# A gated mix of attention and spectral filter: the output bank in two runs of channels, and another order of work at the head

## The chip, the cores and the metric

The kernel runs on one core of a Trainium2 chip. The time is the device time of one execution in microseconds; three runs gave 405.25, 405.87 and 407.12, with a median of 405.87. A profiled execution, from which all rows of the profile come, took 405.76; its span, from the first instruction to the last, is 404.0.

## The reference

Only the input x of branch A is used: both branches read it. `D` is 448, `S` 2048, sixteen heads of 28.

```python
x = A_x
g = _sigmoid((x * gate_w).sum(-1, keepdims=True))
a = _A_ref(x, A_wqkv, A_wo)          # softmax attention, 16 heads of 28
b = _B_ref(x, B_w_r, B_w_i)          # rfft2, times (w_r + 1j*w_i), irfft2, to bfloat16
return g * a + (1 - g) * b
```

```python
qkv = (lambda x, *d: x.transpose(*d))((x @ wqkv).reshape(B, S, 3, H, Dh), 2, 0, 3, 1, 4)
scores = jnp.einsum("bhqd,bhkd->bhqk", q, k) * scale
p = _softmax(scores, axis=-1)
o = jnp.einsum("bhqk,bhkd->bhqd", p, v)
return (lambda x, *d: x.transpose(*d))(o, 0, 2, 1, 3).reshape(B, S, D) @ wo
```

## The kernel before

**Tiling.** Four heads lie on the 128 partitions, each in 32 rows of which 28 hold data. A group is four heads by 512 queries: four groups of heads by four blocks of queries, 16 groups, numbered `n` (`plan_steps`). For each group there are 16 tiles of 128 keys, `kt`. A score tile is one head, one `kt` and 512 queries: `k` times `q` into one PSUM bank. Because the squares of the norms are carried in two spare rows of `q` and `k`, a score is a negative squared distance, and no row maximum is needed; the weights for it are put into `vw`.

**Exponentials.** Most score tiles go to ACT (L1302): three from `psA`, then two from `psB`, into a ring of 28 slots. The list `ND` (L533) says for each group how many of the 16 `kt` go to DVE instead: those are scored into a spare bank (`dunit`, L1250), turned into bit patterns of a power of two by one addition and maximum (L1256), and shifted to three further phases by POOL or DVE (L1268; `PHS[PHX]` says which engine). All four phases are summed by P times V with weights that average them. A tile on ACT costs one P-times-V quad, a tile on DVE four. `pvb` holds the sum over all keys of a group; `normalise` copies it out, inverts the row sums by way of DRAM, and POOL multiplies (L1453).

**Spectral branch** (`background`). It runs beside the attention: a transform over channels (`Bd`), over tokens (`A`, `CS`), the product with the weights, and back. Its result `zt` enters the output tiles.

**Output tiles.** For each of 16 tiles of 128 tokens, `out_mm` (L1462) adds eight terms into one bank: four spectral ones of 224 channels each (even or odd channels, hence a step of two in the bank) and four attention ones, one for each group of heads, with `wo_pad`. DVE copies the bank to `fin` and it goes to DRAM (`out_tile`); the last four tiles are made after the attention's end (`last_tile`), partly beforehand.

**Order.** The program writes out operations with a duration, a key and their dependences; `Sched.run` plays them through and hands out a fixed order for each engine, with due times from the constants at L176 to L194 and `Kernel.T0` to `TB`. PE, ACT, DVE, POOL and the loads on SP each follow their list. POOL operations and those on DVE marked `lk` are kept apart. Where PE would be idle for long, small matmuls of zeros are put in.

**Head** (`prologue`). The constants and the weights of the first four heads' keys go through ACT's queue, the first 512 tokens and the queries' weights through SP's. POOL clears and fills the padded weights `wpk`, DVE fills `wpq`. PE runs 20 matmuls of zeros, transposes the tokens into four banks (copied to `xT` by ACT and DVE in turn), and projects twice: once for the squares (ACT, L841), and once more into another bank, to which a selector matmul adds the norms; DVE scales the sum to `q` and `k` (L852). Queries go first as one piece of 512, keys as pieces of 128 and 384. Blocks 1 to 3 of the keys are made while the first exponentials run: `x_block` transposes, `proj_fast` projects (scale L1032, square L1038, selector matmul, addition L1048), `v_block` makes `vw` and the gate's logits (L1123).

Of the kernel before, what the change touches and what calls it, by code (L numbers as in the profile page):

```python
# [11 lines left out]
BF16 = mybir.dt.bfloat16  # L12
# [9 lines left out]
FN = 113  # L22
# [11 lines left out]
PHX = 1  # L34


def free_dims(ap, dims, offset=0):
    return _AP(tensor=ap.tensor, offset=ap.offset + offset,
               ap=[list(ap.ap[0])] + [list(d) for d in dims])

# [115 lines left out]
class Op:  # L156
    __slots__ = ("first", "last", "heat", "lk", "eng", "dur", "emit", "deps", "key", "rel", "mode", "acq", "free", "lat",
                 "start", "end", "name", "step", "n")
# [23 lines left out]
DUE_P = 7.01  # L182
SWP = 0.98
PVA, PVD = -2, 0.36
URG = 1
FLEAD = 4.66
SQPOOL = 0
EL, ELAST = 1.7, 4.49
NLD = 2
KP = 37.88  # L190
KN, KO, PLEAD, DSP, DHOLD, RWAIT, WREL, XLEAD, QLEAD, WLEAD = 0.77, 4.52, 0.43, 0.54, 2, 1.8, 4, 6.18, 16.76, 5.66
DW, DS = 0.64, 0.4
LDMA, LREM, LRB = 2.46, 2.81, 3.2
DUP = -0.58  # L194
# [6 lines left out]
class Sched:  # L201
# [4 lines left out]
    def op(self, eng, dur, emit, deps=(), key=0.0, rel=0.0, mode=None, acq=None, free=None,  # L206
           lat=None, name=""):
        o = Op(eng, dur, emit, deps, key, rel, mode, acq, free, lat, name)
        self.ops.append(o)
        return o  # L210
# [24 lines left out]
    def close_item(self, o, a):  # L235
        memo = {a: True}

        def inside(x, depth=0):
# [6 lines left out]
            for d in x.deps:  # L245
                if inside(d, depth + 1):
                    r = True
# [217 lines left out]
    def refill(self, order, nb):  # L465
# [24 lines left out]
        busy = [(o.start, o.end, o.heat) for o in pe]  # L490

        def share(a):
            return sum((min(e, a + HAMW) - max(s, a)) * w for s, e, w in busy if s < a + HAMW and e > a) / HAMW
        new = []

        def place(g, most):
# [15 lines left out]
            busy.append((o.start, o.end, 1.0))  # L512
# [19 lines left out]
class Kernel:  # L532
    ND = [0, 3, 3, 4, 2, 3, 3, 3, 4, 3, 3, 4, 3, 4, 2, 4]  # L533
    RING = 28
    T0 = 10.0
    PJE, PJV = 24.12, 19.99
    TA, TB = 47.27, 354.53
# [143 lines left out]
    def plan_steps(self):  # L681
# [24 lines left out]
        for k, st in enumerate(self.steps):  # L706
# [9 lines left out]
            t += 0.052 + 512 * len(st) / 1200.0  # L716
# [4 lines left out]
    def prologue(self):  # L721
# [4 lines left out]
                              (), K0, eng="AQ", dur=0.1, lat=2.6)  # L726
# [3 lines left out]
        self.d_x.append(self.dma(self.xtok[:, 0:4, 0:D], self.x[:, 0:4, :], (), K0, dur=0.45, lat=4.1))  # L730
# [17 lines left out]
        dk = wload(self.wraw0["k"], D, 0, 112, K0 + 1, "AQ", lat=3.9)  # L748
        dq = wload(self.wraw0["q"], 0, 0, 112, K0 + 2, "SP", lat=3.9)
# [18 lines left out]
        def padcopy(w, g, raw, deps, key, eng):  # L768
# [8 lines left out]
            d = 0.28 if eng == "DVE" else 0.45  # L777
            a = sc.op(eng, d, f1, [deps[0], self.pad_ms[w, g]], key, name="padw")
            b = sc.op(eng, d, f2, [deps[1], self.pad_ms[w, g]], key + 0.01, name="padw")
            return [a, b]  # L780
# [11 lines left out]
        for i in range(20):  # L792
            self.pe(256, lambda: self.mm(self.psA[:, 2, 0:256], self.zero[:, 0:P], self.zero[:], True, True),
                    (ms["zero"],), K0 + i * .01, dur=0.175)
# [4 lines left out]
        trs, self.xev = [], {}  # L799
        for c in range(4):  # L800
            n = 113 if c == 3 else 112
            for t in range(4):
                def f(c=c, t=t, n=n):
                    o = homes[c]().bitcast(BF16)[0:n, 128 * t:128 * t + 128]
                    self.tr(o, self.xtok[:, t, CO[c]:CO[c] + 2 * n - 1:2])
                trs.append(self.pe(128, f, (self.d_x[0], self.d_cst, ms["xt"]), K0 + 10 + c, dur=0.056,
                                   acq=(itq, itk)[c - 2] if c > 1 and t == 0 else None))
            eng = "ACT" if c in (0, 2) else "DVE"

            def fe(c=c, n=n, eng=eng):  # L810
# [3 lines left out]
                else:  # L814
                    self.pin(nc.vector.tensor_copy(out=self.xT[0][0:n, c, :], in_=src))  # L815
            self.xev[0, c] = sc.op(eng, 0.36 if eng == "DVE" else 0.55, fe, trs[-4:], K0 + 11 + c, name="xev")
# [5 lines left out]
        parts = (("q", 0, 512, lambda: self.psA[:, 1, :], lambda: self.bgi(itq), itq),  # L822
                 ("k", 0, 128, lambda: self.psB[:, 1, :], lambda: self.bgi(itk), itk),
                 ("k", 128, 512, lambda: self.pv[:], lambda: self.psB[:, 0, :], None))

        def project(b, w, lo, hi, key, stop):
            ops = []
            for c in range(4):
                n = 113 if c == 3 else 112

                def f(c=c, n=n):
# [936 lines left out]
```

## Time and profile before

| what | us |
| --- | --- |
| median of three runs | 405.87 |
| profiled execution, its time | 405.76 |
| its span | 404.0 |
| first exponential starts | 11.88 |
| last exponential ends | 393.85 |

Engines run their own lists at the same time. PE is the matrix engine, ACT the scalar one, DVE the vector one; POOL has the shifted copies and the clearing of tiles; SP issues loads. In a row of the timeline stand the start, the duration, the engine, the line and operation, what is written from what, and in brackets how long the engine had been idle before and what ended that. In a row of the groups stand the count, the total busy time and the mean in nanoseconds. "PE L675" is the line of a helper that all matmuls go through, so matmuls are told apart by their tiles. Instructions of one engine overlap: a start-to-start distance says how fast they follow, a duration how long one takes from end to end.

### The profile page before, as it was taken

What the parts mean: (1) busy time and instruction counts of PE and PEld (TensorE: products, weight loads), DVE (VectorE), ACT (ScalarE), POOL (GpSimd) and SP (SyncE); (2) the same over time, 40 slices, a digit from 0 to 9 for tenths busy, and PEclk for the clock granted to TensorE, in tenths of its full rate; (3) what the DMA queues carried; (4) which work ended last, traced back from release to release, by engine and by line L of the source; (5) the groups of instructions that cost most, each with busy time, mean ns of one, the idle gap of its engine ahead of it and who ended that gap; (6) DMA issues with size and microseconds to landing.
All of it is one profiled execution on the core that took longest, in us unless ns stands there. A gap on an engine that the chain in (4) does not pass through costs nothing.

```text
span 404.0 us, 14729 instructions
## 1 busy us (share of the span) xinstructions
PE 384.8 (95%) x6283; PEld 158.7 (39%) x6283; DVE 304.4 (75%) x580; ACT 383.9 (95%) x352; POOL 277.3 (69%) x248
## 2 busy tenths in 40 slices
PE   8999999999999999999999999999999999999996
PEld 5544333334343333334433333444333443334343
DVE  1554978889888888879797987789898757757652
ACT  3889999999999999999999999999999999999991
POOL 8821285664783667895895897967989995919510
PEclk9999999999999999999999999999999999999999
DMA  8500002220201312121212012112210122122111
GB/s 215 128 3 4 5 18 61 45 54 4 54 26 48 86 41 65 36 58 35 57 46 55 13 35 60 42 46 60 61 34 3 52 78 88 53 79 72 40 26 47
DMA packets 31174, 20.51 MB, mean 51 GB/s; under 512 B 16408, under 2 KB 29188, under 8 KB 31108
## 3 DMA queue, kind: packets, MB, share of 16 engines
q1 hardware_dynamic: 30340, 19.25, 18.5%
q8 instruction: 49, 0.80, 0.9%
q10 hardware_dynamic: 768, 0.32, 0.4%
q14 instruction: 17, 0.14, 0.1%
HBM read 13.67 MB, written 1.97 MB: 39 GB/s over the span
## 4 chain that ended last, share of the span: by engine, by line
ACT 50%; PE 40%; issue 7%; DVE 2%; DVEq 0%; POOL 0%; ACTq 0%; POOLq 0%
ACT ring L1302 50%; PE bg L675 14%; PE pvb L675 11%; PE psA L675 8%; PE psB L675 5%; PE bg L678 1%; ACT w L1084 0%; DVE wpq L776 0%; DVE k L1032 0%; DVE pd L1256 0%; DVE xT L936 0%; DVE X L1716 0%; DVE Ab L1537 0%; DVEq L1763 0%; DVE xT L815 0%
## 5 line engine op out<-in xcount | busy, mean ns | idle before, releaser
L1302 ACT ACTIVATE ring<-psA 128x1536 bf16<-128x1536 f32 x167 | 269.5, 1614 | 5.8 <-PE psA L675 4.3
L1268 POOL TENSOR_SCALAR pd<-pd 128x2048 uint16<-128x2048 uint16 x115 | 216.1, 1897 | 63.1 <-DVE pd L1256 35.0
L1302 ACT ACTIVATE ring<-psB 128x1024 bf16<-128x1024 f32 x166 | 198.3, 1195 | 0.0
L1256 DVE TENSOR_SCALAR pd<-bg 128x512 uint16<-128x512 f32 x192 | 128.4, 685 | 34.4 <-PE bg L675 30.0
L675 PEld LDWEIGHTS <-k 32*128 32x128 bf16 x1024 | 45.9, 91 | 120.8 <-issue 111.7
L675 PE MATMUL pvb<-ring,vw 128*32 128x512 bf16 x832 | 78.2, 385 | 0.4 <-DVE vw L1135 0.2
L675 PE MATMUL psA<-q,k 32*128 32x512 bf16 x500 | 65.6, 382 | 10.1 <-ACT ring L1302 7.1
L675 PE MATMUL bg<-q,k 32*128 32x512 bf16 x192 | 69.7, 381 | 0.3 <-DVE t L1650 0.2
L675 PE MATMUL pvb<-pd,vd 128*32 128x512 bf16 x768 | 69.9, 383 | 0.0
L675 PE MATMUL psB<-q,k 32*128 32x512 bf16 x332 | 65.9, 382 | 2.5 <-ACT ring L1302 1.7
L675 PEld LDWEIGHTS <-vw 128*32 128x32 bf16 x832 | 20.7, 94 | 30.8 <-issue 27.3
L1453 POOL TENSOR_TENSOR q<-pvs,Rb 128x512 bf16<-128x512 f32 x15 | 19.1, 1273 | 16.6 <-PE psB L675 12.3
L675 PEld LDWEIGHTS <-vd 128*32 128x32 bf16 x768 | 19.5, 95 | 21.5 <-issue 17.0
L675 PEld LDWEIGHTS <-xT 112*32 112x32 bf16 x1280 | 20.2, 96 | 9.8 <-issue 9.0
L1268 DVE TENSOR_SCALAR pd<-pd 128x2048 uint16<-128x2048 uint16 x29 | 22.0, 769 | 0.7
L1650 DVE TENSOR_TENSOR t<-bg,Wg 128x450 bf16<-128x450 f32 x32 | 19.0, 619 | 1.8 <-PE bg L675 1.6
L675 PE MATMUL pvb<-zero 128*32 128x256 bf16 (+5 forms) x448 | 19.7, 259 | 0.0
L675 PE MATMUL bg<-xT,wpq 112*32 112x512 bf16 (+2 forms) x244 | 19.4, 383 | 0.0
L675 PEld LDWEIGHTS <-zero 128*32 128x32 bf16 (+1 forms) x504 | 14.2, 98 | 13.1 <-issue 8.1
L675 PE MATMUL bg<-xT,wpk 112*32 112x512 bf16 (+2 forms) x244 | 18.4, 380 | 0.1
L675 PE MATMUL bg<-wo,q 128*32 128x448 bf16 x232 | 17.9, 364 | 0.1
L675 PE MATMUL bg<-Bd,X 113*32 113x224 bf16 x240 | 15.9, 379 | 0.0
(124 smaller groups left out, 363.2 us busy)
## 6 DMA issues: line engine op xcount, KB each, us to landing
Rb<-rsc SPq DMA_DIRECT2D x60, 64.0 KB
CS<-cCS SPq DMA_DIRECT2D x16, 192.0 KB
xtok<-Ab SPq DMA_DIRECT2D x16, 112.5 KB
V<-xtok SPq DMA_DIRECT2D x16, 112.5 KB
xtok<-in_A_x_dram SPq DMA_DIRECT2D x4, 448.0 KB
out_dram<-fin SPq DMA_DIRECT2D x12, 112.0 KB
Wg<-in_B_w_r_dram SPq DMA_DIRECT2D x32, 28.1 KB
Wg<-in_B_w_i_dram SPq DMA_DIRECT2D x32, 28.1 KB
```

Of the source, the lines that this page charges most:

```text
L675: self.pin(self.nc.tensor.matmul(out, lhsT=lhsT, rhs=rhs, start=start, stop=stop, **kw))
L678: self.pin(self.nc.tensor.transpose(out=out, in_=in_, identity=self.c("ident")[0:n, 0:n]))
L1256: self.pin(nc.vector.tensor_scalar(out=ys[:, s, :].bitcast(U16), in0=self.bgi(it), scalar1=127 * UNITS, scalar2=0.0, op0=ALU.add, op1=ALU. ...
L1268: self.pin(e.tensor_scalar(out=fl(pds), in0=fl(ys), scalar1=float(PHASE[f]), scalar2=1.0, op0=ALU.add, op1=ALU.mult))
L1302: self.pin(nc.scalar.activation(out=self.ring[:, u0:u0 + len(st), :], in_=slot[:, 0:len(st), :], func=ACT.Exp, scale=LN2 / UNITS))
L1453: e = self.pool(1.15, lambda: self.pin(nc.gpsimd.tensor_tensor(out=dst, in0=pvs[:], in1=self.Rb[:], op=ALU.mult)), ds, kk)
L1650: self.pin(nc.vector.tensor_tensor(out=out[:], in0=self.bgi(it)[:, 0:F2].rearrange("p (a f) -> p a f", a=2), in1=free_dims(Wg[:], [[F - 2 ...
```

## The change

Eight things change in the code.

- The four spectral terms of an output tile are written as two runs of 224 channels, even channels first. The copies to `fin` interleave them (`pairs` writes with a step of two, `halves` reads the runs). `wo` is loaded into the two `fin` buffers and rearranged into `wo_pad` by POOL to fit.
- `ND` sums to 50 instead of 48: 824 tiles on ACT instead of 832. `PHX` is 3 instead of 1: of four tiles, one has a phase on DVE, instead of one of two.
- The first 512 tokens come in two loads, one on SP's queue and one on ACT's, and the transposes run half by half. The second block of tokens is loaded ahead of the first value weights.
- 15 matmuls of zeros instead of 20 at the start.
- Keys come first, in two halves of 256: DVE scales the projection, a selector matmul makes the norms in the other half of the same bank, DVE adds. Queries follow; ACT scales one half and DVE the other.
- Clearing the other heads' padded weights, `vw[1]` and `vd`, is held back until the first key weights are ready, or until a release time.
- Half of the transposes of token blocks 2 and 3 go to the bank `pvb`.
- The planner's constants and its model of an exponential's duration are others.

```diff
-PHX = 1
+PHX = 3
...
-    ND = [0, 3, 3, 4, 2, 3, 3, 3, 4, 3, 3, 4, 3, 4, 2, 4]
+    ND = [0, 4, 3, 3, 3, 2, 4, 3, 3, 4, 3, 3, 3, 4, 4, 4]
...
-            t += 0.052 + 512 * len(st) / 1200.0
+            t += EX0 + EX1 * len(st)
...
-        self.d_x.append(self.dma(self.xtok[:, 0:4, 0:D], self.x[:, 0:4, :], (), K0, dur=0.45, lat=4.1))
+        self.d_x.append([self.dma(self.xtok[:, 0:2, 0:D], self.x[:, 0:2, :], (), K0, dur=0.45, lat=3.2),
+                         self.dma(self.xtok[:, 2:4, 0:D], self.x[:, 2:4, :], (), K0 + .5, eng="AQ", dur=0.5, lat=3.4)])
...
-            m1 = self.pool(0.5, lambda t=t: self.pin(nc.gpsimd.memset(t[:], 0.0)), (), key)
+            m1 = self.pool(0.5, lambda t=t: self.pin(nc.gpsimd.memset(t[:], 0.0)),
+                           () if g == 0 else self.wready["k", 0], key, rel=26.0 if g else 0.0)
...
-        for i in range(20):
+        for i in range(15):
...
+        p1k = project(self.psB[:, 1, :], "k", 0, 256, K0 + 20, True)
+        p1q = project(self.psA[:, 1, :], "q", 0, 512, K0 + 21, True)
+        p1l = project(self.pv, "k", 256, 512, K0 + 25, True)
+        for i, b, lo, hi, p1 in ((0, self.psB[:, 1, :], 0, 256, p1k), (2, self.pv, 256, 512, p1l)):
+            a = square(i, b, lo, hi, p1)
...
+                self.pin(nc.vector.tensor_scalar(out=kq[:, lo:hi], in0=b[:, lo:hi], scalar1=sv, scalar2=None, op0=ALU.mult))
...
+                self.mm(b[:, 256 - lo:512 - lo], self.c("selk"), self.sq[:, 512 * i + lo:512 * i + hi], True, True)
...
+                self.pin(nc.vector.tensor_tensor(out=kq[:, lo:hi], in0=b[:, 256 - lo:512 - lo], in1=kq[:, lo:hi], op=ALU.add))
...
+                        if eng == "ACT":
+                            self.pin(nc.scalar.activation(out=o, in_=b, func=ACT.Copy, scale=sv))
+                        else:
+                            self.pin(nc.vector.tensor_scalar(out=o, in0=b, scalar1=sv, scalar2=None, op0=ALU.mult))
...
+            self.wod.append([self.pool(0.65, lambda g=g, st=st: self.pin(nc.gpsimd.tensor_copy(
+                out=halves(self.wo_pad[g][:]), in_=pairs(st[:]))), ds, 152 + g)])
...
+            inpv = half == 0 and b in XPV
...
-            self.mm4(bank[:, (0, 1, 1, 0)[k]:D:2], self.zt[0:FN, t, 128 * k:128 * k + 128],
+            self.mm4(bank[:, 224 * (0, 1, 1, 0)[k]:224 * (0, 1, 1, 0)[k] + 224], self.zt[0:FN, t, 128 * k:128 * k + 128],
...
-        e = self.dve(0.55, lambda: self.pin(nc.vector.tensor_copy(out=fin[:], in_=self.bgi(it)[:, 0:D])),
+        e = self.dve(0.55, lambda: self.pin(nc.vector.tensor_copy(out=pairs(fin[:]), in_=halves(self.bgi(it)[:, 0:D]))),
```

More of the change, by code (lines that the diff above doesn't have):

```diff
@@ L1 @@
+from bisect import bisect, insort
 from contextlib import ExitStack
@@ L511, in place @@
             new.append(o)
-            busy.append((o.start, o.end, 1.0))
+            insort(busy, (o.start, o.end, 1.0))
             g[0] = o.end
```

164 lines of the change are left out of this document (91 added, 73 removed).

## The prediction

> **What bounds the kernel now.** First the page: engine totals, the chain that ended last, the costliest groups.
>
> ```profile
> PE 384.8 (95%) x6283; PEld 158.7 (39%) x6283; DVE 304.4 (75%) x580; ACT 383.9 (95%) x352; POOL 277.3 (69%) x248
> ...
> ACT 50%; PE 40%; issue 7%; DVE 2%; DVEq 0%; POOL 0%; ACTq 0%; POOLq 0%
> ...
> L1302 ACT ACTIVATE ring<-psA 128x1536 bf16<-128x1536 f32 x167 | 269.5, 1614 | 5.8 <-PE psA L675 4.3
> L1268 POOL TENSOR_SCALAR pd<-pd 128x2048 uint16<-128x2048 uint16 x115 | 216.1, 1897 | 63.1 <-DVE pd L1256 35.0
> ```
>
> ACT's exponentials hold half of the chain, PE most of the rest. They alternate: three score tiles from psA, two from psB; I call this pair a cycle and number it from 0. Their durations overlap, so the pace is read from starts. The timeline of ACT, one row each for cycles 0, 4, 5, 6, 7, 139 and 165 and for the last two steps:
>
> ```profile
> 11.88 1.45 ACT L1302 ACTIVATE ring<-psA 128x1536 bf16<-128x1536 f32 x1 [2.20 <-PE psA L675]
> ...
> 21.64 1.45 ACT L1302 ACTIVATE ring<-psA 128x1536 bf16<-128x1536 f32 x1 [0.53 <-PE psA L675]
> ...
> 23.89 1.46 ACT L1302 ACTIVATE ring<-psA 128x1536 bf16<-128x1536 f32 x1
> ...
> 27.51 1.45 ACT L1302 ACTIVATE ring<-psA 128x1536 bf16<-128x1536 f32 x1 [1.18 <-PE psA L675]
> ...
> 29.76 1.46 ACT L1302 ACTIVATE ring<-psA 128x1536 bf16<-128x1536 f32 x1
> ...
> 328.86 1.45 ACT L1302 ACTIVATE ring<-psA 128x1536 bf16<-128x1536 f32 x1
> ...
> 390.56 1.46 ACT L1302 ACTIVATE ring<-psA 128x1536 bf16<-128x1536 f32 x1
> 391.89 1.04 ACT L1302 ACTIVATE ring<-psB 128x1024 bf16<-128x1024 f32 x1
> 392.79 1.06 ACT L1302 ACTIVATE ring<-psA 128x1024 bf16<-128x1024 f32 x1
> ```
>
> Four stretches. The head ends at 11.88. Cycles 0 to 6 take 15.63 us, 2.6 a cycle, with gaps that PE ends. From cycle 7 to 139, 132 cycles take 299.10 us: 2.266 each, with ACT never idle. From 139 to the last step at 392.79, 27 cycles take 63.93: 2.368 each. The rest is the tail, from the last exponential's end (393.85) to 404.0: 10.15 us. The stretches by engine (length, then busy time and count of PE, PEld, DVE, ACT, POOL, then clock and DMA) show what slows the fourth:
>
> ```profile
> 300.00:330.00 30.00, 28.81 (x476) 12.17 (x469) 22.27 (x40) 29.95 (x27) 28.65 (x20) 1.00 0.14 40
> 330.00:360.00 30.00, 29.95 (x541) 11.90 (x529) 20.16 (x34) 29.17 (x27) 18.93 (x13) 1.00 0.23 69
> 360.00:393.85 33.85, 33.44 (x568) 13.39 (x560) 22.88 (x37) 32.87 (x29) 17.65 (x11) 1.00 0.19 56
> ```
>
> There ACT has holes and PE is full: the output tiles are made there. So ACT bounds the middle, PE the end, data the first seven cycles.
>
> **Fewer exponentials.** ND's sum goes from 48 to 50: 832 score tiles on ACT become 824, eight more go to DVE. Instead of 166 full cycles and a two-tile step there are 164, a triple and a single. A triple step is 1.33 us of pace (390.56 to 391.89); for the last single I take 0.62, below the pair's 1.06. From cycle 6 that is 2 x 2.266 - (1.33 + 0.62 - 1.06) = 3.6 us less. It counts in full only if PE, DVE and POOL keep up. DVE gets eight L1256 more and eleven L1268 fewer:
>
> ```profile
> L1268 DVE TENSOR_SCALAR pd<-pd 128x2048 uint16<-128x2048 uint16 x29 | 22.0, 769 | 0.7
> ...
> L1256 DVE TENSOR_SCALAR pd<-bg 128x512 uint16<-128x512 f32 x192 | 128.4, 685 | 34.4 <-PE bg L675 30.0
> ```
>
> 8 x 0.685 - 11 x 0.769 = -3.0 us: no load. POOL gets 17 copies more (115 to 132, PHX = 3): 17 x 1.897 = 32.2 us on 277.3, against 63.1 us idle before such copies. Counted in the changed instruction order, all copies but those around cycle 21 have 3 us or more between the release of their buffer and their reader, beyond the POOL work between; and at 28.65 of 30 us busy (300 to 330) ACT still ran at 29.95. I take nothing; the upper bound is the third rival's.
>
> **Output bank in two runs.** The first two groups write 224 columns with a step of two, the third 226 side by side, four at a time on the four column tiles:
>
> ```profile
> L675 PE MATMUL bg<-Bd,X 113*32 113x224 bf16 x240 | 15.9, 379 | 0.0
> ...
> L675 PE MATMUL bg<-Bd,xT 112*32 112x226 bf16 x256 | 10.1, 263 | 0.1
> ```
>
> ```profile
> 327.12 0.93 PE L675 MATMUL bg<-Bd,X 113*32 113x224 bf16 x16
> ```
>
> ```profile
> 61.23 0.58 PE L675 MATMUL bg<-Bd,xT 112*32 112x226 bf16 x16
> ```
>
> Four quads end to end: (0.93 - 0.379) / 3 = 0.184 us each with the step, (0.58 - 0.263) / 3 = 0.106 without. 64 quads (16 tiles by four) save 64 x 0.078 = 5.0 us of PE, nearly all after 326. The excess there is 27 x (2.368 - 2.266) = 2.75 us, so 5.0 covers it; ND[14] from 2 to 4 puts back eight quads of P times V for two, six of 512 columns at 0.106 x 512 / 226 = 0.24: 1.4 us. Gain 2.75; bounds 0 and 3.0. The interleaved write moves to the copies on DVE and ACT: L1494 copies 448 in 0.62, and a copy that writes runs of 28 takes the same,
>
> ```profile
> L1494 DVE CAST fin<-bg 128x448 bf16<-128x448 f32 x12 | 7.4, 621 | 7.7 <-PE bg L675 7.6
> ...
> L1135 DVE TENSOR_TENSOR vw<-bg,w 128x448 bf16<-128x448 f32 x13 | 8.0, 617 | 1.5 <-PE bg L675 1.4
> ...
> L773 POOL COPY wpk<-X 112x224 bf16<-112x224 bf16 x4 | 1.4, 371 | 1.2 <-DVE sq L1038 1.1
> ...
> L942 DVE COPY xT<-bg 112x512 bf16<-112x512 bf16 x3 | 1.3, 418 | 0.2 <-PE bg L678 0.2
> ```
>
> so nothing; at worst double, 12 x 0.62 on a DVE with a quarter free, and 0.6 in the tail. Rearranging wo costs POOL four copies of 448 (0.37 for 224, hence 0.75 each) and two memsets in place of four; this lies near 60 to 100 us, long before the first output tile. The 16 loads of wo go through SP as before. Nothing.
>
> **The head.**
>
> ```profile
> 1.10 4.45 PE L675 MATMUL psA<-zero 128*128 128x256 bf16 x20 [1.10 <-POOL zero L751]
> ...
> 2.20 1.28 ACT L790 ACT_TABLE_LOAD   x1 [2.20 <-issue]
> ...
> 5.34 0.63 PE L678 MATMUL psB<-cst,xtok 128*112 128x128 bf16 x4
> ...
> 6.19 0.76 PE L678 MATMUL bg<-cst,xtok 128*112 128x128 bf16 x8
> ```
>
> ```profile
> 5.62 0.22 DVE L773 COPY wpq<-X 112x224 bf16<-112x224 bf16 x1 [5.62 <-DMA X<-in_A_wqkv_dram]
> ...
> 6.78 0.94 DVE L776 COPY wpq<-X 112x224 bf16<-112x224 bf16 x1
> 6.99 0.72 DVE L815 COPY xT<-bg 113x512 bf16<-113x512 bf16 x1
> ...
> 10.28 0.75 DVE L852 TENSOR_SCALAR q<-bg,cst 128x512 bf16<-128x512 f32 x1 [2.56 <-PE bg L675]
> ```
>
> PE goes from warm-up to transposes without a gap, so the warm-up held them. Twenty took 5.34 - 1.10, 0.212 each; fifteen end at 4.28. Half of x should be there (the whole of it lies ahead of the weights that landed by 5.62). ACT issues a load more ahead of the key weights and of its table load; the table would be in by about 4.0 instead of 3.48 and is not used before the first xT copy. Sixteen transposes at 0.106 end near 6.1 instead of 6.9, and the 0.94 copy, beside POOL's memsets that now come later, falls back to 0.22. So keys and queries are projected 0.8 to 1.0 sooner. Afterwards it is a longer chain: DVE's key scaling waits for ACT's square, and DVE's half of the query for ACT's half (both waits stand in the changed order), some 0.85 for the 0.75 above. First exponential: 10.9; bounds 10.3 and 11.9. The Trainium skill (PSUM — Partial Sum Buffer, "PSUM bank collisions raise a hardware error") lets no two engines access one bank and quadrant at once; run side by side, the halves would give about 10.5, and by the page they cannot.
>
> But cycles 0 to 6 wait for keys, not for the start:
>
> ```profile
> 24.14 0.75 DVE L1032 TENSOR_SCALAR k<-bg,cst 128x512 bf16<-128x512 f32 x1 [0.55 <-PE bg L675]
> ...
> 24.92 0.42 DVE L1038 TENSOR_TENSOR sq<-k 128x512 bf16<-128x512 bf16 x1
> ...
> 26.19 0.68 DVE L1048 TENSOR_TENSOR k<-bg,k 128x512 bf16<-128x512 f32 x1
> ...
> 27.02 0.39 PE L675 MATMUL psA<-q,k 32*128 32x512 bf16 x3
> ```
>
> Cycle 6 needs key block 2. Before, scale (24.14), square, one xT copy and the addition (to 26.87) precede the score. In the changed order DVE's addition stands behind scale 0.75, square 0.42, gate logits 0.16, vw 0.62 and two xT copies of 0.41, and PE's selector quad behind three P-times-V quads that wait for that vw. Cycle 4 waits for block 1's addition as before (about 21.5), cycle 5 starts at 23.75; then: last xT copy 23.95, scale 25.15 to 25.9, square 26.3, logits and vw 27.05, three quads 27.75, selector 28.2, addition 28.9, score, exponential 29.4. That is 1.9 later than 27.51: the start's gain is spent and more. Bounds 26.9 (wait of cycle 5 no longer than before) and 31.
>
> **Tail.** The tile of psA that lies ahead of the last row sums has four quads without the step (-0.3). POOL's last q copy (1.27) now follows DVE's last copies more closely and PE needs it 0.8 after them (+0.4), and tiles 12 and 13 leave a quad more at the end (+0.15): +0.25, bounds -0.4 and +0.8.
>
> **Sum**, against the profiled run of 405.76 (span 404.0 and 1.76 around it; median 405.87): -3.6 - 2.75 + 1.9 + 0.25 = -4.2: span 399.8, time 401.5.
>
> **Rivals.**
> Head faster as a whole: cycle 6 at 26.9. For: four kernel stretches of xT now use the idle pv bank. Against: the DVE order above. 401.5 - 2.5 = 399.0. Chance 0.17.
> End not relieved: something else (DVE copies, late rows) keeps 2.37 a cycle there. For: PE is full; against: counted in the changed order, no stretch of 14 cycles holds more PE work than 29.4 us, 2.1 a cycle. 401.5 + 2.75 = 404.25, about the same time. Chance 0.15.
> Slower: POOL becomes the bound. Place: the last three groups, ND 4, 4, 4; 23 copies fall into cycles 140 to 160, 43.6 us plus two q copies of 1.27 against 20 x 2.266 = 45.3.
>
> ```profile
> POOL pd L1268 <- DVE pd L1256: 35.0, 14, 9.6
> POOL pd L1268 <- DVE pd L1268: 16.5, 9, 5.3
> ```
>
> These waits (51.5) may not shrink; then the 32.2 us find only 63.1 - 51.5 = 11.6, 20.6 come up as late P times V, and half of that behind buffers gives +10: 411.5. It decides from 6.4 us unhidden on (407.9). Against: the slack counted above. Chance 0.12.
> Clock: the transposes took 314 ns to psB and pass to a 0.07 pace only after 6.19, so PE was slow until then. With five warm-up matmuls fewer and a gap before the second half of x, the slow pace could last through the projections, eight matmuls of 512 at 0.43 instead of 0.21: +1.7 on the start, about +1 at cycle 6: 402.5. Chance 0.08. The Trainium skill (TensorE: Matmul & The Clock Gate, "Part 1: The HAM clock gate") says just that: full clock after a busy window of some 3.4 us; the rows agree with it.
>
> **Chances.** Forecast 0.48 (398.5 to 404). The rivals as given. Faster by over 0.5% (below 403.84; 0.5% is about what a measurement can tell from no change): forecast nearly whole, head, clock and a little of the end: 0.69. Within: 0.19. Slower: 0.12. The range for eight in ten: 397 (best head, no end loss) to 407 (end not relieved, cycle 6 at 31).
>
> **What would show it.** First exponential 10.3 to 11.9; cycle 6 near 29.4 with a PE-ended gap of 2 to 3 us; 165 triples; 2.27 a cycle after 330; output matmuls of 224 near 262 ns; POOL at 305 to 312 us. PE waiting for POOL by more than 3 us would prove me wrong, as would a first stretch shorter than before.

## The result, and the profile after

The changed kernel takes 401.52 us, median of four runs (401.24 to 401.61), where the kernel before takes 405.75 beside it: a ratio of 0.9889, 95% interval 0.9865 to 0.9914. The profiled execution took 401.59, its span is 399.8 (before: 404.0). Forecast were 401.5 and a span of 399.8.

The page first: engine totals, the chain that ended last, and the two groups that the change of ND moves.

```profile
PE 377.1 (94%) x6262; PEld 155.2 (39%) x6262; DVE 306.2 (77%) x579; ACT 379.8 (95%) x350; POOL 309.5 (77%) x267
...
ACT 52%; PE 35%; issue 7%; DVE 3%; DMA 1%; ACTq 0%; POOL 0%; DVEq 0%; POOLq 0%
...
L1309 POOL TENSOR_SCALAR pd<-pd 128x2048 uint16<-128x2048 uint16 x132 | 247.7, 1898 | 39.5 <-DVE pd L1297 20.7
L1343 ACT ACTIVATE ring<-psA 128x1536 bf16<-128x1536 f32 x165 | 271.4, 1645 | 4.8 <-PE psA L689 4.8
```

There are 165 triples, and POOL is at 309.5 with 132 copies (277.3 + 32.2): the forecast's numbers. Its idle time before these copies is down from 63.1 to 39.5. The share of PE in the chain fell from 40% to 35%. DMA stands there with 1% that it did not have.

The timeline of ACT, for the same cycles as before (0, 4, 5, 6, 7, 139, the last triple, and the single behind it):

```profile
12.17 1.45 ACT L1343 ACTIVATE ring<-psA 128x1536 bf16<-128x1536 f32 x1 [0.73 <-PE psA L689]
...
22.30 1.45 ACT L1343 ACTIVATE ring<-psA 128x1536 bf16<-128x1536 f32 x1 [0.61 <-PE psA L689]
...
24.61 1.47 ACT L1343 ACTIVATE ring<-psA 128x1536 bf16<-128x1536 f32 x1
...
30.28 1.45 ACT L1343 ACTIVATE ring<-psA 128x1536 bf16<-128x1536 f32 x1 [3.28 <-PE psA L689]
32.60 1.47 ACT L1343 ACTIVATE ring<-psA 128x1536 bf16<-128x1536 f32 x1
...
331.27 1.65 ACT L1343 ACTIVATE ring<-psA 128x1536 bf16<-128x1536 f32 x1
...
387.79 1.66 ACT L1343 ACTIVATE ring<-psA 128x1536 bf16<-128x1536 f32 x1
389.12 0.82 ACT L1343 ACTIVATE ring<-psB 128x512 bf16<-128x512 f32 x1
```

The end is relieved: from 139 to 164, 25 cycles take 56.52, 2.261 each, the pace of the middle. The head is worse than forecast: the first exponential starts at 12.17 (10.9 forecast, 11.9 the upper bound), cycle 6 at 30.28 behind a wait of 3.28 for PE (29.4 and a wait of 2 to 3 were forecast). The windows of the last three stretches (length, then busy time and count of PE, PEld, DVE, ACT, POOL, clock, DMA) say the same of the end: ACT has no holes any more, and PE has a little room.

```profile
300.00:330.00 30.00, 28.35 (x501) 12.26 (x501) 21.70 (x36) 30.00 (x27) 29.37 (x19) 1.00 0.20 56
330.00:360.00 30.00, 29.12 (x512) 11.36 (x504) 21.43 (x36) 30.00 (x28) 26.94 (x18) 1.00 0.25 70
360.00:389.94 29.94, 29.50 (x482) 11.38 (x482) 23.23 (x37) 29.94 (x28) 21.05 (x13) 1.00 0.13 39
```

For the experiments it is useful to cut the span at cycles 0, 12 and 139 and at the last exponential. The numbers in this table are starts of exponentials on ACT or differences of them; "last one" is the duration of the last exponential, and the tail is the span less its end. The profiled execution of the run named "block 2 early" (417.09 us) was disturbed from cycle 48 on, so it is read to cycle 12 alone, where the listed clock is 1.00.

| profiled run | cycle 0 | 0 to 6 | 6 to 12 | 12 to 139 | 139 to last | last one | tail |
|---|---|---|---|---|---|---|---|
| before | 11.88 | 15.63 | 13.81 | 287.54 | 63.93 | 1.06 | 10.15 |
| after | 12.17 | 18.11 | 13.56 | 287.43 | 57.85 | 0.82 | 9.86 |
| step of two put back | 12.43 | 18.10 | 13.54 | 288.67 | 60.22 | 0.62 | 10.52 |
| ND[13] less two | 12.00 | 18.11 | 13.56 | 287.76 | 61.05 | 1.21 | 10.01 |
| before, output bank alone | 11.01 | 15.63 | 13.81 | 287.55 | 61.02 | 1.25 | 9.63 |
| old head | 11.82 | 18.46 | 13.48 | 289.23 | 59.45 | 0.67 | 12.59 |
| block 2 early | 11.47 | 15.44 | 16.00 | not read | not read | | |
| second block's load moved, order kept | 11.27 | 18.10 | 13.54 | 287.45 | 57.84 | 0.83 | 9.87 |
| the same, query in one piece | 11.03 | 18.12 | 13.54 | 287.45 | 57.81 | 0.83 | 9.82 |
| the same, selector first | 10.88 | 17.89 | 14.31 | 287.37 | 57.82 | 0.83 | 9.80 |

From before to after: +0.29 at the start, +2.48 and -0.25 in the first twelve cycles, -0.11 in the middle, -6.08 behind cycle 139, -0.24 for the shorter last step, -0.29 in the tail: -4.2.

### The profile page after: what moved, and what is told of

Read it like the earlier page. It is cut to its first block, busy times and chain, and to the rows that moved or that the text cites. A ratio compares the mean times of both kernels' runs of the same rounds, so it can differ in the third digit from the quotient of the medians.

```text
span 399.8 us, 14715 instructions
## 1 busy us (share of the span) xinstructions
PE 377.1 (94%) x6262; PEld 155.2 (39%) x6262; DVE 306.2 (77%) x579; ACT 379.8 (95%) x350; POOL 309.5 (77%) x267
## 3 DMA queue, kind: packets, MB, share of 16 engines
q1 hardware_dynamic: 30084, 19.02, 18.1%
## 4 chain that ended last, share of the span: by engine, by line
ACT 52%; PE 35%; issue 7%; DVE 3%; DMA 1%; ACTq 0%; POOL 0%; DVEq 0%; POOLq 0%
ACT ring L1343 51%; PE bg L689 13%; PE pvb L689 10%; PE psA L689 7%; PE psB L689 5%; DMA X<-in_A_wqkv_dram 1%; DVE vw L1176 0%; PE bg L692 0%; DVE q L1017 0%; ACTq L664 0%; DVE pd L1297 0%; DVE t L1691 0%; DVE k L1073 0%; DVE k L1017 0%; DVE sq L1027 0%
## 5 line engine op out<-in xcount | busy, mean ns | idle before, releaser
L1309 POOL TENSOR_SCALAR pd<-pd 128x2048 uint16<-128x2048 uint16 x132 | 247.7, 1898 | 39.5 <-DVE pd L1297 20.7
L1343 ACT ACTIVATE ring<-psB 128x1024 bf16<-128x1024 f32 x165 | 201.3, 1220 | 0.0
L1297 DVE TENSOR_SCALAR pd<-bg 128x512 uint16<-128x512 f32 x200 | 134.2, 686 | 32.0 <-PE bg L689 28.9
L689 PE MATMUL psA<-q,k 32*128 32x512 bf16 x495 | 64.9, 381 | 10.9 <-ACT ring L1343 7.6
L689 PE MATMUL bg<-q,k 32*128 32x512 bf16 x200 | 73.4, 382 | 0.0
L689 PE MATMUL pvb<-pd,vd 128*32 128x512 bf16 x800 | 72.0, 382 | 0.4
L689 PE MATMUL bg<-xT,wpq 112*32 112x512 bf16 (+1 forms) x240 | 18.2, 383 | 0.0
L689 PE MATMUL bg<-xT,wpk 112*32 112x512 bf16 (+1 forms) x240 | 17.7, 383 | 0.2 <-DVE xT L986 0.2
L1129 POOL CAST vw<-w 128x16 bf16<-128x16 f32 (+1 forms) x7 | 2.3, 347 | 17.8 <-ACT w L1125 15.1
L1309 DVE TENSOR_SCALAR pd<-pd 128x2048 uint16<-128x2048 uint16 x18 | 13.9, 787 | 0.4
```

What stands on the lines that cost most here:

```text
L689: self.pin(self.nc.tensor.matmul(out, lhsT=lhsT, rhs=rhs, start=start, stop=stop, **kw))
L1129: self.pin(nc.gpsimd.tensor_copy(out=free_dims(self.vw[g][:], [[32, 16 * nb]], 4 * b0 * 128 + DH), in_=free_dims(self.w[g][:], [[1, 16 * n ...
L1297: self.pin(nc.vector.tensor_scalar(out=ys[:, s, :].bitcast(U16), in0=self.bgi(it), scalar1=127 * UNITS, scalar2=0.0, op0=ALU.add, op1=ALU. ...
L1309: self.pin(e.tensor_scalar(out=fl(pds), in0=fl(ys), scalar1=float(PHASE[f]), scalar2=1.0, op0=ALU.add, op1=ALU.mult))
L1343: self.pin(nc.scalar.activation(out=self.ring[:, u0:u0 + len(st), :], in_=slot[:, 0:len(st), :], func=ACT.Exp, scale=LN2 / UNITS))
```

## The experiments

### Fewer exponentials

```diff
-PHX = 3
+PHX = 1
-    ND = [0, 4, 3, 3, 3, 2, 4, 3, 3, 4, 3, 3, 3, 4, 4, 4]
+    ND = [0, 3, 3, 4, 2, 3, 3, 3, 4, 3, 3, 4, 3, 4, 2, 4]
```

> The changed kernel with the score tiles shared out as before (ND and PHX of before: 832 tiles on ACT). My theory: the middle and the end are paced by ACT's exponentials at 2.26 us a cycle, so two cycles more (less the partial steps) cost 3.6 us: span near 403.4, time near 405.1, PE then with more room. Rival: the new tuning constants of the order carry the gain and the share does not matter: within 0.5 us of the changed kernel's 401.5.

408.58 us (408.08 to 411.38), 7.1 longer, and neither theory's number. Cycle 69 takes 5.99 us instead of 2.26: the planner worked out another order for the whole kernel, and this one has a stall there. The edit can't be read from the total, but it can be read behind cycle 139, where this profile has 61.09 to the last start and a last exponential of 1.17, together 3.59 more than the changed kernel. The next edit leaves the order nearly alone.

```diff
-    ND = [0, 4, 3, 3, 3, 2, 4, 3, 3, 4, 3, 3, 3, 4, 4, 4]
+    ND = [0, 4, 3, 3, 3, 2, 4, 3, 3, 4, 3, 3, 3, 2, 4, 4]
```

> The changed kernel with one entry of ND put down by two: the fourteenth, 4 to 2. Eight score tiles go back from DVE to ACT, 832 there as before; nothing else is edited, so that the stall that the first try of this (all of ND and PHX as before) had at cycle 69 should not come. My theory: ACT paces the kernel from cycle 6 on, so the price is 2 x 2.263 less the partial steps, 3.6 us at the most; cycle 6 to the last exponential's end 3.2 to 3.6 longer, time 404.8 to 405.5. Rival: what the exponentials cost is had back at the end, where PE then has fewer P-times-V quads: 1.5 us or less.

405.75 us (405.35 to 408.11), 4.2 longer, a little above the 405.5 expected at most. In the profile, cycle 139 and the last step (ACT's timeline):

```profile
331.43 1.65 ACT L1343 ACTIVATE ring<-psA 128x1536 bf16<-128x1536 f32 x1
...
392.48 1.21 ACT L1343 ACTIVATE ring<-psA 128x1024 bf16<-128x1024 f32 x1
```

From 139 to the last start it is 61.05 where the changed kernel has 57.85, and the last exponential is 0.39 longer: 3.59. The forecast term was 3.6. The rest of the difference is 0.33 between cycles 12 and 139 (cycle 69 takes 2.78 here) and 0.15 in the tail. The rival, 1.5 or less, falls.

### The output bank

The step of two, put back into the changed kernel; nothing that the planner sees is different, so every engine keeps its order.

```diff
-            self.mm4(bank[:, 224 * (0, 1, 1, 0)[k]:224 * (0, 1, 1, 0)[k] + 224], self.zt[0:FN, t, 128 * k:128 * k + 128],
+            self.mm4(bank[:, (0, 1, 1, 0)[k]:D:2], self.zt[0:FN, t, 128 * k:128 * k + 128],
...
-                out=halves(self.wo_pad[g][:]), in_=pairs(st[:]))), ds, 152 + g)])
+                out=self.wo_pad[g][:], in_=st[:])), ds, 152 + g)])
```

(The three copies out of the bank lose `pairs` and `halves` in the same way.)

> The changed kernel with the output bank of before: the first two groups written with a step of two, plain copies out of it, wo staged without the rearrangement. My theory: 64 quads take 0.184 us again instead of 0.106, 5.0 us of PE behind 326 us; the end is full, so the pace there goes from 2.26 back to 2.35 to 2.37 a cycle: +2.0 to +2.75, time 403.5 to 404.3. Rival: with fewer exponentials and another order PE has room there, and the step costs less than 0.5 us.

405.82 us (405.32 to 407.51): 4.3 longer, all of the change's gain. ACT's timeline at cycles 139 and 164 and the single step:

```profile
332.74 1.45 ACT L1343 ACTIVATE ring<-psA 128x1536 bf16<-128x1536 f32 x1 [0.32 <-PE psA L689]
...
391.63 1.46 ACT L1343 ACTIVATE ring<-psA 128x1536 bf16<-128x1536 f32 x1
392.96 0.62 ACT L1343 ACTIVATE ring<-psB 128x512 bf16<-128x512 f32 x1
```

25 cycles in 58.89: 2.356 each, as expected, and PE ends the waits again. The price is higher than expected for two reasons: 1.24 is lost between cycles 12 and 139 too (the first output tiles fall into cycles 134 to 138), and the tail is 0.66 longer.

The same edit alone, in the kernel before. To keep its order, the rearranged wo was made by eight POOL copies put behind eight of its pd copies, not by operations of their own in the plan.

```diff
+        at = [o for o in order if o.eng == "POOL" and o.name == "dexp" and o.start > 130.0][:24:3]
+        for i, o in enumerate(at):
+            def f(i=i, was=o.emit):
+                was()
+                w, st = self.wo_pad[i // 2][:], self.fin[i // 2 % 2][:]
+                a, b = (st, w) if i % 2 == 0 else (halves(w), pairs(st))
+                self.pin(self.nc.gpsimd.tensor_copy(out=a, in_=b))
+            o.emit = f
```

> The kernel before with the output bank in two runs and nothing else, every engine's order kept: the copies out of the bank interleave, and wo is rearranged by eight POOL copies put behind eight of its pd copies after 130 us. Theory (the prediction's term): the pace behind cycle 139 falls from 2.368 to 2.27 a cycle, 2.4 to 2.75, with 0.3 in the tail: 402.5 to 403.2. Rival (from the changed kernel with the step put back, 4.3 longer): the edit is worth 4 us here too, 401.3 to 401.9. Third: POOL's eight copies more delay its pd copies, and the gain is under 1.5.

402.00 us (401.43 to 402.60) beside 405.68, ratio 0.9910 (0.9891 to 0.9930): 3.7 less, between the theory's number and the first rival's. The groups, and ACT's timeline at cycles 139 and 165 and the last step:

```profile
L691 PE MATMUL bg<-Bd,X 113*32 113x224 bf16 x240 | 10.2, 261 | 0.0
...
L1510 DVE CAST fin<-bg 128x448 bf16<-128x448 f32 x12 | 8.0, 667 | 5.9 <-PE bg L691 5.8
```

```profile
328.00 1.66 ACT L1318 ACTIVATE ring<-psA 128x1536 bf16<-128x1536 f32 x1
...
386.78 1.65 ACT L1318 ACTIVATE ring<-psA 128x1536 bf16<-128x1536 f32 x1
389.02 1.25 ACT L1318 ACTIVATE ring<-psA 128x1024 bf16<-128x1024 f32 x1
```

The 224-column matmul takes 261 ns (379 before), the copies that interleave 667 (621). Behind cycle 139 the 27 cycles take 61.02 instead of 63.93, 2.260 each; with the last exponential, which is 0.19 longer, and 0.52 less in the tail, this is 3.24. Between cycles 0 and 139 the two profiles agree to 0.01, but as the sum of two parts: this run is 0.37 behind at cycle 137, all of it lost between cycles 55 and 76, while POOL makes its eight extra copies (whether they cause it isn't shown), and wins 0.36 back in cycles 137 and 138, where the first output tiles are made. So the step by itself is worth 3.6 in the profile. The profiles also differ by 0.87 at the start, which no part of this edit touches (11.01 here, 11.88 before).

### The head: what made it late

Key weights ahead of the second half of x on ACT's queue:

```diff
-        dk = wload(self.wraw0["k"], D, 0, 112, K0 + 1, "AQ", lat=3.2)
+        dk = wload(self.wraw0["k"], D, 0, 112, K0 + .2, "AQ", lat=3.2)
```

> The changed kernel with one load moved: the key weights are issued on ACT's queue ahead of the second half of the first tokens. My theory of the late first exponential (12.17 where I had 10.9): the key weights land late because they are issued behind that half; moved ahead, POOL's two copies of them start near 5.5 and 6.0 instead of 6.23 and 7.35, the first exponential comes at 11.2 to 11.5, and cycle 6 follows only in part (29.4 to 30). Rival: the transfers share the DMA engines, the second half of x then comes as much later as the keys come earlier, and the first exponential stays within 0.2 us of 12.17.

410.16 us (408.65 to 411.07). The key copies do start at 4.38 and 4.97, and the first exponential at 15.57: 3.4 later, against both theories. PE's timeline shows the wait and what follows it, ACT's the first exponential, and the window of 9 to 12 the clock that the profile lists (1.00; the last section says why):

```profile
6.55 0.46 PE L692 MATMUL psB<-cst,xtok 128*112 128x128 bf16 x2 [1.22 <-DMA xtok<-in_A_x_dram]
...
9.35 1.91 PE L689 MATMUL psA<-xT,wpq 112*128 112x512 bf16 x4
...
12.97 0.63 PE L689 MATMUL psA<-sq,cst 128*128 128x512 bf16 x1
```

```profile
15.57 1.45 ACT L1343 ACTIVATE ring<-psA 128x1536 bf16<-128x1536 f32 x1 [0.92 <-PE psA L689]
```

```profile
9.00:12.00 3.00, 2.53 (x9) 1.04 (x8) 0.91 (x2) 0.98 (x2) 0.00 (x0) 1.00 1.13 287
```

The transposes of the second half of x start 1.4 us later than in the changed kernel (6.55 for 5.13), PE idles 1.22, and then the 512-column matmuls follow at (1.91 - 0.63) / 3 = 0.43, the slow pace of the prediction's clock rival. To tell the clock from the transfers, zeros were multiplied in the gap:

```diff
+            if h == 0:
+                for i in range(14):
+                    self.pe(256, lambda: self.mm(self.psA[:, 2, 0:256], self.zero[:, 0:P], self.zero[:], True, True),
+                            (ms["zero"], trs[3][1]), K0 + 13.5 + i * .01, dur=0.01)
```

> The run with the key weights first (first exponential at 15.57, PE idle for 1.22 us ahead of the second half of the first tokens, and matmuls of 512 at 0.43 apart behind it), with 14 matmuls on zeros put between the two halves of the transposes, so that PE does not idle there. My theory, the rival that I gave 0.08 in the prediction: that gap takes PE back to the slow pace, and this is nearly the whole delay; with the gap filled the 512-column matmuls follow at 0.22, and the first exponential comes at 12.4 to 13.0. Rival: the delay is that of the transfers (the second half of x lands 1.4 later); then it stays at 14.8 or later.

```profile
5.12 2.16 PE L689 MATMUL psA<-zero 128*128 128x256 bf16 x14
...
7.12 0.28 PE L692 MATMUL psB<-cst,xtok 128*112 128x128 bf16 x2
...
8.94 1.03 PE L689 MATMUL psA<-xT,wpq 112*128 112x512 bf16 x4
```

```profile
13.10 1.45 ACT L1347 ACTIVATE ring<-psA 128x1536 bf16<-128x1536 f32 x1 [0.73 <-PE psA L689]
```

(1.03 - 0.38) / 3 = 0.22, and the first exponential at 13.10, just above the expected band: 2.47 of the 3.40 were the pace of PE. The 0.93 that is left can't be put down to the transfers alone: the second half of x was transposed from 6.55 in the run with the gap, while here the zeros themselves hold PE until 7.12. Total 407.25 (406.24 to 408.85), 2.9 less than with the gap. Both totals hold stalls of 1.3 to 1.4 and 1.1 at cycles 36 and 42 and a tail 2.8 longer, behind the new order that the planner made for the moved load; they say nothing about the head. (Cycle 36 lies in a stretch for which the profile lists a clock of 0.50, 98.34 to 105.16 in the run with the gap and 98.24 to 101.65 here.)

The second block's load behind the value weights, as before the change:

```diff
-        self.wvd = {0: self.wload(self.wv0, 2 * D, 0, 112, -4988.5, "SP", lat=5.0) + gs}
+        self.wvd = {0: self.wload(self.wv0, 2 * D, 0, 112, -4989.5, "SP", lat=5.0) + gs}
```

> The changed kernel with the load of the second token block (448 KB) issued behind the value weights on SP's queue again, as before the change. Theory: what made the key weights late is this transfer, moved up beside them; without it POOL's second key copy starts 0.7 to 1.2 earlier than 7.35 and the first exponential comes at 11.2 to 11.6 instead of 12.17. Rival: it is their place behind the second half of x on ACT's own queue (or the value weights take the same room): POOL's second copy stays within 0.3 of 7.35.

404.94 us (403.70 to 406.01): 3.4 longer, with a tail of 12.45 from a new order. But the second key copy starts at 6.39 and the first exponential at 11.37, 0.8 earlier. With the order kept and the three loads alone exchanged:

```diff
+        loads = [self.d_x[1]] + self.wvd[0][:2]
+        loads[0].emit, loads[1].emit, loads[2].emit = loads[1].emit, loads[2].emit, loads[0].emit
```

> The changed kernel with every engine's order kept as it is, only that on SP's queue the load of the second token block is issued behind the two loads of the value weights instead of ahead of them (the run before with that load moved had another order in the tail as well, 2.6 us longer). Theory: in the runs with the changed head the first exponential stands 4.82 us behind the start of POOL's second key copy (7.35 and 12.17 in the changed kernel), and this copy waits for a transfer that shares the time with those 448 KB; here it starts at 6.3 to 6.6, the first exponential comes at 11.2 to 11.5, and all that follows is earlier by the same: 0.5 to 0.9 off the changed kernel's time. Rival: the first twelve cycles hold their end in place whatever the start; less than 0.2.

400.75 us (400.62 to 401.04), ratio to before 0.9881 (0.9862 to 0.9900): 0.77 less than the changed kernel. POOL's second key copy and the first exponential here, then the same copy in the changed kernel:

```profile
6.18 0.37 POOL L794 COPY wpk<-X 112x224 bf16<-112x224 bf16 x1
...
11.27 1.45 ACT L1345 ACTIVATE ring<-psA 128x1536 bf16<-128x1536 f32 x1 [0.73 <-PE psA L691]
```

```profile
7.35 0.37 POOL L792 COPY wpk<-X 112x224 bf16<-112x224 bf16 x1 [0.75 <-DMA X<-in_A_wqkv_dram]
```

And in the kernel before:

```profile
6.02 0.37 POOL L776 COPY wpk<-X 112x224 bf16<-112x224 bf16 x1
```

With the loads exchanged the copy no longer waits for the transfer. Loads do not land at the same time in every run: in five profiles with the changed kernel's loads this copy starts at 6.65 to 7.60, and the first exponential each time 4.82 or 4.83 behind it (11.47 to 12.43). The 11.27 here and the 11.37 of the run before are below all five.

### The head: the query's two halves

In the changed kernel DVE's half waits for ACT's, a wait that the prediction had found in the changed order (the timelines of ACT and DVE):

```profile
10.69 0.47 ACT L887 ACTIVATE q<-psA,cst 128x256 bf16<-128x256 f32 x1 [1.01 <-PE psA L689]
...
11.20 0.48 DVE L889 TENSOR_SCALAR q<-psA,cst 128x256 bf16<-128x256 f32 x1 [1.30 <-ACT q L887]
```

```diff
-                        o, b = self.q[0][:, x:x + 256], self.psA[:, 0, x:x + 256]
-                        if eng == "ACT":
-                            self.pin(nc.scalar.activation(out=o, in_=b, func=ACT.Copy, scale=sv))
-                        else:
+                        o, b = self.q[0][:, 0:512], self.psA[:, 0, 0:512]
+                        if eng == "DVE":
```

> The run with the second block's load behind the value weights, order kept, and the query of the first scores scaled by one instruction on DVE (512 columns, 0.75) instead of 256 on ACT and then 256 on DVE (0.47 and 0.48, one behind the other). Theory: the two halves never ran side by side, so one piece is 0.2 to 0.25 faster to the first score: first exponential 0.2 to 0.25 earlier against the second key copy (4.6 instead of 4.82), and as much off the whole. Rival: DVE's key scaling and the second half's keys queue behind the longer instruction and the first key waits of cycles 3 and 4 grow by as much: no change.

400.48 us (400.32 to 400.85), the fastest version of this study: ratio to before 0.9873 (0.9854 to 0.9892). PE's row of the second half of the key projection and the first exponential, here and then without the edit (there the first exponential is at 11.27):

```profile
6.82 0.38 PE L691 MATMUL psB<-xT,wpk 112*128 112x256 bf16 x2
...
11.03 1.45 ACT L1343 ACTIVATE ring<-psA 128x1536 bf16<-128x1536 f32 x1 [0.60 <-PE psA L691]
```

```profile
6.89 0.38 PE L691 MATMUL psB<-xT,wpk 112*128 112x256 bf16 x2
```

The step from the key projection's second half on PE to the first exponential is 4.21, where it was 4.38: 0.17, a little less than expected. The first exponential is still 4.82 behind the second key copy (4.6 expected), but here that copy is not what it waits for. The waits of cycles 0 to 6 did not grow (18.12 for 18.10), so the rival falls. The medians differ by 0.27, and the ranges of the two versions overlap (400.62 to 401.04 without it), so the trace shows the gain and the times alone would not settle it.

### The head: cycles 0 to 12

```diff
-        self.d_x.append([self.dma(self.xtok[:, 0:2, 0:D], self.x[:, 0:2, :], (), K0, dur=0.45, lat=3.2),
-                         self.dma(self.xtok[:, 2:4, 0:D], self.x[:, 2:4, :], (), K0 + .5, eng="AQ", dur=0.5, lat=3.4)])
+        self.d_x.append(self.dma(self.xtok[:, 0:4, 0:D], self.x[:, 0:4, :], (), K0, dur=0.45, lat=4.1))
...
-        for i in range(15):
+        for i in range(20):
...
-XPV = (2, 3)
+XPV = ()
...
-FLEAD = 3.34
+FLEAD = 4.66
```

> The changed kernel with the whole head of before: one load of the first tokens, the old order of loads and memsets, 20 warm-up matmuls, queries and keys scaled as before, no xT in the pv bank, and the old leads of key blocks 1 to 3. My theory: the new head is a loss of 2 to 2.8 us at cycle 6, so here the first exponential is near 11.9, cycle 6 near 28 instead of 30.3, time 399 to 399.7. Rival: the new head is what lets the rest be packed; then cycle 6 is no earlier than 29.8 or the loss shows later, time 401 or more.

406.37 us (406.00 to 408.50). The first exponential is at 11.82, as before, and cycle 6 at 30.28, to the hundredth where the changed kernel has it:

```profile
30.28 1.45 ACT L1320 ACTIVATE ring<-psA 128x1536 bf16<-128x1536 f32 x1 [4.64 <-PE psA L689]
```

So the new prologue is not what delays cycle 6. Nor is the share of tiles or the output bank by itself: in the profiles with either put back, cycle 6 stands 18.10 behind cycle 0. That leaves the planner's other constants as the likeliest to have placed the work there; no run put those back by themselves. The total says nothing of the head: behind it the new order has stalls of 1.7 and 1.5 us at cycles 32 and 159 (the second where the listed clock is 0.50, from 378.05 to 381.46), and a tail of 12.59.

```diff
-                self.x_block(b, due - XLEAD - XB * (b - 1))
+                self.x_block(b, due - XLEAD - XB * (b - 1) - (0, 0, 2, 2)[b])
```

> The changed kernel with the xT of blocks 2 and 3 given 2 us more lead, which puts block 2's scale, square and addition on DVE one right behind the other. Cycle 6 should start at 26.9 to 27.4 instead of 30.28. Theory of the prediction: the place of that addition is what the head loses; cycle 12 then comes 2 us or more earlier than in the changed kernel. Rival: the first twelve cycles hold more work for PE and DVE than ACT takes for them, so what is taken from block 2's wait comes back at block 3's (cycles 9 and 11), and cycle 12 is within 0.5 us of the changed kernel's. The order behind is another too, so this is read at cycle 12, not at the end.

407.38 to 407.74 us (three of four executions), with another order behind the head. Cycles 0, 6 and 12:

```profile
11.47 1.45 ACT L1343 ACTIVATE ring<-psA 128x1536 bf16<-128x1536 f32 x1 [0.73 <-PE psA L689]
...
26.91 1.45 ACT L1343 ACTIVATE ring<-psA 128x1536 bf16<-128x1536 f32 x1 [1.29 <-PE psA L689]
...
42.91 1.45 ACT L1343 ACTIVATE ring<-psA 128x1536 bf16<-128x1536 f32 x1
```

Cycle 6 is 2.67 nearer to the start than in the changed kernel, cycle 12 only 0.23: 2.44 come back at cycles 9 and 11. The prediction's theory of the place falls, the rival holds. Once more, without a new order: on top of the fastest version the selector quad (a quad is four matmuls on the four column tiles) was put ahead of the three P-times-V quads, and the three scores of cycle 6 ahead of two quads of block 3's projection.

```diff
+        i = j = order.index(self.selk[2])
+        n = 0
+        while n < 3:
+            j -= 1
+            if order[j].eng == "PE":
+                n += 1
...
+        order.insert(j, order.pop(i))
+        i = j = next(i for i, o in enumerate(order) if o.name == "score" and o.step == 12)
+        n = 0
+        while n < 2:
+            j -= 1
+            n += order[j].eng == "PE"
+        order.insert(j, order.pop(i))
```

> The run with the query in one piece, and on PE, around key block 2 alone, two things moved with every other engine's order kept: the selector quad of block 2 ahead of the three P-times-V quads that wait for the same vw, and the three scores of cycle 6 ahead of the last two quads of block 3's projection. From the changed kernel's rows the addition can start at 28.46 (end of the last xT copy) instead of 29.03, so cycle 6 stands 17.5 to 17.7 behind the first exponential instead of 18.12. Theory of the prediction (the head loses where block 2 stands in the queues): the 0.5 us stay, cycle 12 and the end are earlier by as much, time 399.9 to 400.2. Rival (what block 2 gains, block 3 loses): cycle 12 and the time stay within 0.15 us of that run's 400.5.

400.73 us (400.62 to 401.74): no gain, and 0.25 more than the run without it, a little beyond the rival's 0.15. Cycles 5 to 8:

```profile
23.63 1.47 ACT L1359 ACTIVATE ring<-psA 128x1536 bf16<-128x1536 f32 x1
...
28.77 1.45 ACT L1359 ACTIVATE ring<-psA 128x1536 bf16<-128x1536 f32 x1 [2.75 <-PE psA L705]
...
31.55 1.45 ACT L1359 ACTIVATE ring<-psA 128x1536 bf16<-128x1536 f32 x1 [0.34 <-PE psA L705]
...
34.06 1.45 ACT L1359 ACTIVATE ring<-psA 128x1536 bf16<-128x1536 f32 x1
```

Cycle 5 to 6 is 5.14 (5.68 without), so the 0.54 are won, and cycle 6 to 12 takes 14.31 instead of 13.54: 0.77 given back. (0.31 more was lost ahead of cycle 5, where PE waited 0.54 for the second block's tokens: a price that moving their load can have. Of the other three profiles with it moved one shows 0.19 of such a wait.) The windows of cycles 5 to 8, before and after, show what is in the stretch:

```profile
23.89:32.06 8.17, 7.78 (x159) 3.97 (x155) 3.82 (x8) 7.00 (x9) 0.51 (x2) 1.00 0.01 2
```

```profile
24.61:34.83 10.22, 9.62 (x239) 5.15 (x239) 6.78 (x14) 6.94 (x9) 6.36 (x23) 1.00 0.01 3
```

PE is nearly full in both, 95% and 94%, and the changed order puts 9.62 us of it between the same cycles instead of 7.78: 1.84 of the 2.05 by which the stretch is longer. By lines the difference is work for later: key projections 44 matmuls instead of 20, values 128 instead of 64, query projections 16 instead of none. DVE and POOL have more there too (6.78 for 3.82, 6.36 for 0.51), but are busy for 66% and 62% of it; PE waits for DVE for 0.79 of it. Over all twelve cycles PE has 1.27 more (29.13 for 27.86) of the 2.23 by which they are longer, and the rest is more idle time of PE. This fits the rival: whoever goes first in such a stretch, the last score of it comes when PE is through.

## Why the prediction was right, point by point

**Fewer exponentials: -3.6.** Measured 3.59, behind cycle 139, in two runs. Mechanism and size as forecast. POOL took the 17 copies; PE waited for it nowhere behind the head, so the slower rival fell by its own mark. The waits of POOL for DVE that this rival thought might not shrink (51.5) fell to 26.5.

**Output bank: -2.75 at the end, -0.3 in the tail.** Measured alone -2.72 (61.02 + 1.25 against 63.93 + 1.06) and -0.52, and 0.36 more ahead of cycle 139: 3.6. Put back into the changed kernel the step costs 4.1 in the profile, where it reaches back to cycle 134. So the two main terms help each other by about half a microsecond; the prediction took them as independent. Behind cycle 139 the changed kernel has eight P-times-V matmuls more (320 for 312) in 6.3 us less, which may be the reason; no run shows it. The copies out of the bank, put at nothing, do cost more with the interleaving (0.67 for 0.62 on DVE): the rows of runs of 28 that the prediction took for a likeness are another pattern.

**The head: +1.9 at cycle 6.** Measured +2.77 there, +2.52 at cycle 12. This is the term that was mis-sized, and its two parts were off in opposite ways. The sentence "So keys and queries are projected 0.8 to 1.0 sooner" failed: it followed the transposes and the warm-up, which did end early, and did not cost the order of the loads. Behind the second half of x and beside 448 KB of the second block the key weights came 1.3 later than before (second copy at 7.35 instead of 6.02), and the first exponential was 1.27 later than forecast. Moving one load behind two others brought 0.9 of that back: 11.27, and 0.77 us of the total. The other 0.4 stays with that load moved. The step from the first exponential to cycle 6, 18.5 forecast, was 18.1. The chain behind it ran as written (block 2's scale at 25.98, the addition at 29.03), but the reason given, its place on DVE, was only where the delay showed. Put forward, it gains 0.23 by cycle 12 in one run and nothing in the other. What stretches the head is, by the two windows and the two moves, most likely the PE work placed between cycles 5 and 8; no run took that work out of the stretch, so it isn't shown.

**Tail: +0.25.** Measured -0.29: the step's part is -0.52 instead of -0.3, and what is left for POOL's last q copy and the quad more is 0.23 instead of 0.55 (a remainder, not measured by itself). The head with the middle came to +2.41 (2.52 - 0.11), 0.5 more than the +1.9, and the tail was 0.54 less than forecast. These two errors cancel, so that the total of 401.5 came out to the last half microsecond is luck.

**The clock rival, 0.08.** It did not come: in the changed kernel the transposes run on without a gap, and the queries' projections of 512 columns stand 0.22 apart. But it is real, and 1.2 us of waiting were enough to call it up. So the change's order of loads on ACT's queue, x ahead of the keys, is what its shorter warm-up needs; it is the second block's load that stood in the wrong place. **The query's halves** ran one after the other, as forecast, because DVE is made to wait for ACT; one piece is faster by 0.17. No run lets them go side by side, so what the bank would do then isn't shown.

## What to carry to other kernels

Read an edit by stage, and keep the order when you test it: of six edits that let the planner work anew, four brought stalls or a tail of 1 to 4 us behind the stage that they were meant for, and a fifth (block 2 early) was 6 us longer in all, while the edits made behind the plan left the sums of all other stages the same to 0.1 us. Where an operation is late in a stretch in which an engine is full, moving it forward moves the wait; look at what else was put into the stretch. When a head is rebuilt, cost its transfers first: which load is behind which, on the queue and on the engines that they share.

## What the hardware showed that I had not expected

The slow pace of PE does not show in the listed clock: in the run with the gap it reads 1.00 from 9 to 12 us, where matmuls of 512 stand 0.43 apart, twice the later 0.22. The trace's clock record, from which that column is made, begins only with the step to the full clock, and ahead of its first entry the column reads 1.00. That entry stands at 5.76 us in the changed kernel, at 6.08 in the run with the gap filled, and at 16.42 in the run with the gap: there PE was slow from its first matmul to 16.42, although it was busy for most of that time. The Trainium skill (TensorE: Matmul & The Clock Gate, "Part 1: The HAM clock gate") says that PE is given its full clock after a busy window of some 3.4 us and loses it after an idle one of the same length. The first half agrees with all 14 profiles here: stretches at full clock last a multiple of 3.413 us (392.53 is 115 of them), and PE was busy for 99% or more of the 3.41 us ahead of the first entry. In the run with the gap the three stretches of that length before the last one hold 0.84, 0.41 and 0.47 us of idle PE: the gap lies across the first two, and a wait for ACT at 11.48 in the third. So 1.2 us of waiting, and a short wait after it, cost three stretches; this is one run. The second half does not fit as it stands: in the same run the listed clock falls to 0.50 at 98.34, and PE was busy for 86% of the 3.41 us ahead of that.

A copy of 448 on ACT that writes with a step of two elements takes 0.66 us where the plain one takes 0.53 (in the run with the step put back), and on DVE 0.67 instead of 0.62: the interleaving that PE was relieved of costs the copies 0.05 to 0.13 a tile, and had cost PE four quads at 0.078, 0.31 a tile.
